# A hand-ordered attention and MLP kernel on one core: the opening and batches 1 to 4 in a new order

## The chip, the cores and the metric

The kernel runs on one core of a Trainium2 chip. The metric is device time in microseconds (us), from several executions; a profiled execution of the same program gives the trace that is read below. In a profile's lines PE is TensorE's matmul, PEld its weight load, DVE VectorE, ACT ScalarE, POOL GpSimd, and SPq the DMAs that SyncE issues.

## The reference

x is (8 batches, 8 heads, 512 tokens, 64), state (8, 8, 32, 64). Each batch and head attends both ways between tokens and state rows, and the results are joined and put through an MLP:

```
scores = scale * np.matmul(x, state.transpose(0, 1, 3, 2))
a = np.exp(scores - scores.max(-1, keepdims=True)); a /= a.sum(-1, keepdims=True) + 1e-09
xread = np.matmul(a, state)
scores2 = scale * np.matmul(state, x.transpose(0, 1, 3, 2))
a2 = ...                                  # the same softmax over the tokens
sread = np.matmul(a2, x)
y = np.concatenate([xread, sread], axis=2)   # then heads side by side: (8, 544, 512)
xn = (y - mu) / np.sqrt(var + 1e-06) * g_ln
out = y + np.maximum(xn @ w_ch1, 0.0) @ w_ch2    # 512 -> 2048 -> 512
```

## The kernel before

**Numbers.** Products run in float16 on TensorE. Each factor is split in a high and a low half (ScalarE writes the high one with an activation, VectorE the low one with one scalar_tensor_tensor), and three products of halves (TERMS) are summed. The weights come as 64-bit words, two int32 each; `words` (L653 and L697 load them, 1 MB a tile, through SyncE's queue) turns them into float32 on ScalarE and VectorE. Since xread is a product of the weights of attention with the state, the first layer is taken as state times w1 first (`state_products`, L756 for batches 0 and 1, L750 for the others; its result is the tile "matrix"), and the attention's numerators ("ea") times that.

**Batch 0** is the opening. TensorE turns x and the state (L379), scores them (L439), and ScalarE, VectorE and GpSimd take the softmax, while the weights are loaded, converted and scaled. The hidden layer is done in four units of 512 columns. `first_products` (L810) gives each unit's hidden values, `second_products_by_unit` (L824) multiplies them with that unit's w2. For units 0 to 2 the result of two of the four row blocks goes through ScalarE into a tile "part", and an accumulating DMA, issued by GpSimd, adds it to the residual xr in SBUF. There are two of these DMAs to a unit, six in all. `differences` prepares a unit's w2 for the later batches: GpSimd makes a tile d from w2h in three operations, then ScalarE and VectorE each write half of the result into w2h.

**Batches 1 to 7.** `attention(b)` loads x and state, splits x into float16 halves (tile x16, "x" in the profile) in four pieces, and turns state and x with DMA transposes that SyncE issues (sT, then xT in two halves, later ebT). `products(b)` then does the MLP with fewer, combined products (L903, L913, L961).

**Buffers.** A tag names a ring of buffers in SBUF. "quad" has two, and these serve in turn the part tiles, the tile d, and others (the state rows s_r, eB, ts, ef). "rows" and "halves" have two each. In PSUM there are four accumulators (acc), one pair of banks and two halves. A tile that takes a buffer waits until everything that used its predecessor is through, an accumulating DMA that reads it included.

**Order.** Every piece of the kernel is a generator that yields single instructions, or a group of matmuls, as closures made by `do` (L194). So nearly all instructions are recorded at L198; the matmul helpers and the loads of weights have lines of their own. The generators stand in one list of streams: 0 gain, 1 attention(0), 2 to 5 weights1 of the four units, 6 state_products(0), 7 first_products, 8 to 11 weights2, 12 to 15 sums_of_weights, 16 common_scale, 17 to 20 second_products_by_unit, 21 to 24 differences, 25 attention(1), 26 state_products(1), 27 to 30 halves_of_weights, 31 to 48 products(1), 49 attention(2), and so on to 178. PLAN (L42 to L169) is one long text of items `stream:step` or `stream:first-last`, and `issue` walks it:

```python
with tc.manual_schedule():
    for item in plan.split() or [...]:
        k, n = item.split(":")
        n = [int(v) for v in n.split("-")]
        for f in streams[int(k)][n[0]:n[-1] + 1]:
            f()
```

Each engine executes its instructions in the order in which they were issued here, and semaphore waits keep what depends on each other in order across engines. A tile gets its ring buffer where its first step stands in PLAN. So PLAN sets the order on each engine, SyncE's and GpSimd's DMAs included, and which tiles share a buffer.

Of the kernel before, what the change touches and what calls it, by code (L numbers as in the profile page):

```python
# [42 lines left out]
    "0:0 1:7 1:6 1:5 1:4 1:8 1:13 1:1 1:19 1:0 4:0 0:3 1:14 1:3 1:15 1:9 0:4 1:16 1:10 1:17 1:2 0:5 1:18 1:11 1:23 "  # L43
    "4:2 1:21-22 4:3 1:20 1:24 2:0 4:1 2:3 4:4 0:6 1:27-28 1:12 0:2 2:2 1:25 1:29 1:41 1:26 4:6 2:4 4:5 1:30 1:33 "
    "1:67 1:34 2:1 0:1 1:42 3:0 1:31 4:7 1:36 2:5 1:32 4:8 1:43-45 1:48 2:6 3:3 3:1 2:7 1:35 1:46 4:12 4:9 2:8 1:37 "
    "4:10-11 3:2 3:4 3:6 1:49 3:5 1:47 4:13 5:0 2:12 2:10 3:7 1:39 3:8 1:38 5:1 5:6 9:1 1:50 2:9 5:2 25:1 5:5 1:55 "
    "2:11 1:60 1:51 3:11 1:61 3:10 4:14 3:9 2:13 3:12 5:3 2:14 3:13 1:52 8:1 1:62 4:15 1:70 1:68 2:15 1:71-72 1:53 "
    "25:0 2:16 3:14 1:69 5:7 8:5 2:17 1:57 1:54 3:15 25:10 1:73-74 2:18 3:16 1:75 2:19 1:56 1:63-64 3:17 9:0 25:8 "
    "5:4 3:18 1:65 6:0 6:3 6:1 3:19 9:5-6 1:40 6:5 6:2 1:78 6:8 6:4 7:0 4:16 8:0 6:6 1:58 6:9 6:7 8:2 1:87 8:6 9:7 "
    "7:18 1:88 8:3 7:1 1:83 8:7 25:9 1:59 25:5 9:3 25:11 8:4 5:8 7:2 7:19 9:2 1:84 7:20 8:8 9:4 1:89 1:85 25:2 25:6 "  # L50
    "25:3 1:90 25:13 9:16 25:12 7:3 25:14 5:12 25:15 1:86 9:17 8:16 9:8 8:9 5:10 8:17-18 7:9-10 5:11 25:16 8:10-11 "
    "9:18 5:9 4:17 8:12 1:91 7:4-5 10:1 7:6 25:17 9:9 8:13 7:11 8:14 25:18 5:13 1:92 7:7 1:93 9:10 1:94 1:76 5:14 "
    "7:8 8:19 1:95 9:11 1:79 10:6 25:19 7:21 25:21 10:5 9:12 1:96 10:0 5:15 8:20 9:13 1:77 7:22 8:15 1:80-81 7:15 "
    "9:14 7:12 25:24 25:26 5:16 7:23 7:16 25:29 25:20 25:25 17:3 7:13 25:30 10:7 7:14 17:1 25:4 17:6 10:2-4 1:82 "
    "25:7 25:34 9:19 7:17 9:15 1:97 17:0 17:4 10:8 25:27 11:1 25:22 9:20 4:18 25:35 17:2 17:8 11:5 25:31 10:9 "
    "11:6-7 10:10 17:7 17:5 18:6 17:9 11:0 18:0 10:11 25:32 4:19 11:3 10:12 11:2 6:10 12:4 6:11 11:4 6:13 18:8 13:2 "
    "6:12 11:8 17:10 10:13 12:5 25:23 25:28 10:15 21:1 18:7 5:17-18 18:1 6:14 18:9 11:9-10 6:15 13:4 11:11 21:0 "
    "1:66 12:2 21:2 10:14 13:5 5:19 26:0 11:12-13 11:15 16:0-1 21:3-4 10:19 25:73 18:2 16:2 18:10 16:4 13:3 18:3 "
    "10:20 26:4 6:18 18:4 12:0 7:27 49:2 25:33 6:19 26:5 12:1 7:24 26:6 6:16 11:14 7:28-29 27:0 7:25 7:33 18:5 7:34 "
    "11:16 7:26 25:36 6:17 27:1 7:30 13:0 7:35 19:1 25:38 10:16 7:31 10:17-18 12:3 25:39 14:4 49:3 14:2 14:5 19:3 "  # L60
    "7:32 14:0 25:40 19:0 25:41-42 49:1 14:3 14:1 25:37 25:43 49:0 19:4 7:36 25:48 26:7 25:49 7:37 26:8 13:1 7:45 "
    "7:42 7:38 26:9 19:2 11:17 25:50 19:6 26:1 25:51-52 25:44 25:53 19:5 11:18 7:43 26:2 25:54 7:44 19:8 11:19-20 "
    "7:46-47 20:6 7:39 27:2 25:60-61 19:9 27:9 19:7 26:3 25:62 27:10 25:55 20:0 25:56 31:0 25:57 49:10 25:58 49:12 "
    "27:11 7:40 31:5 31:2 7:41 20:3 31:1 23:0 49:11 25:45 31:4 49:9 31:3 31:7 27:3-4 23:1 49:8 27:5 23:2 25:46 31:6 "
    "23:3-4 19:10 20:1 25:47 25:59 49:13 20:4 49:14 31:8 49:15 31:11 31:9 28:3 31:10 33:0 22:0 31:13 49:4 33:2 49:6 "
    "20:2 49:16 22:1 49:17-19 33:4 49:31 49:24 20:8 22:2 49:26 26:10 31:14 28:4 20:9 20:7 49:25 33:5 33:1 22:3 "
    "26:11 33:3 33:7 31:12 20:10 49:32 28:5 32:0 49:29-30 32:1 33:6 49:5 22:4 33:10 33:8-9 33:13 49:27 32:2 24:1 "
    "35:0 33:11 26:12 15:2 33:14 35:1 25:68 35:5 32:3 34:3 33:12 35:3 34:0 25:63 49:21 15:4 15:0 35:8 35:7 35:9 "
    "34:1 35:11 25:70 35:2 29:6 49:7 24:0 29:7 35:4 24:2 35:6 29:8 25:69 35:12 35:10 25:67 25:64 34:2 28:9-10 15:1 "
    "37:0 37:2 37:1 37:3 15:5 37:5-6 28:11 37:4 35:13 36:0 35:14 29:0 40:0 37:8 37:7 29:1 24:3 36:2-3 40:1 15:3 "  # L70
    "24:4 40:3 37:11-12 37:10 36:1 37:9 29:2 40:2 40:4 25:66 49:22 25:65 25:71 25:74 28:0 25:75 40:5 49:23 37:13-14 "
    "28:1 40:6 28:2 38:1 25:76 40:7 29:3 40:10 49:34 29:4 25:80 49:28 49:35 38:0 49:20 42:0 25:77 42:1 40:8-9 39:1 "
    "29:5 39:2 49:73 40:13-14 49:33 38:2 39:4-5 42:5 42:3 28:6 42:7 69:2 38:3 28:7 41:0 39:6 42:6 28:8 42:11 42:2 "
    "42:4 40:11-12 49:36 42:10 49:38 41:3 44:0-1 42:8-9 49:37 42:12 49:39 41:1 25:72 49:48 44:5 41:2 44:3 39:3 "
    "42:13 44:7 44:9 42:14 43:2 49:49 43:1 49:40-42 44:8 25:82-83 49:50 49:43 49:51 25:81 49:44 44:2 27:6 50:3 27:7 "
    "20:5 44:6 49:52 44:10 43:0 27:8 50:4 44:11 43:3 46:0 44:4 44:13 46:5 49:53 46:2 46:1 29:9 50:5 46:6 49:54 46:3 "
    "49:60 45:0 46:8 44:14 45:3 50:0 46:10 49:61 69:4 46:4 49:62 46:7 49:64 50:1 29:10 49:45 50:2 29:11 25:84 46:11 "
    "46:9 44:12 49:65 30:6-7 47:0 45:2 49:67 25:78 46:12-13 45:1 49:70 50:6-7 51:0-1 25:85 49:46 50:8 51:2 51:4 "
    "47:1 30:8 49:69 25:79 51:5 49:66 46:14 25:86 51:6 30:3 47:3 51:3 25:87 51:8 49:68 49:55 69:5 25:88 49:47 51:7 "
    "49:56 47:2 51:10 49:57-59 39:0 51:9 49:63 53:0 39:7 48:0 39:8 48:1 30:4 49:71 51:13 53:5 53:2 51:14 53:1 48:3 "  # L80
    "53:8 49:74 51:11 52:0 49:75 53:6 69:3 69:0 30:5 53:3 51:12 49:76 53:4 52:3 69:1 69:9 48:4 55:0 30:9 48:2 69:7 "
    "69:11 69:10 55:1 48:5 52:2 53:10 53:7 69:12 30:10 69:8 53:9 55:5 30:11 49:77 48:6 30:0 69:13-14 49:80 52:1 "
    "69:15 53:11 69:16 30:1 69:17 49:84 39:9 53:12 69:18 55:2 49:72 69:19 55:6 55:10 30:2 55:3 54:0 69:31 53:13-14 "
    "54:1 50:9 54:2 55:8 55:7 55:4 69:32 54:3 69:21 69:6 69:24 50:10 56:0 50:11 49:81 57:0 69:22 55:11 49:85 "
    "69:29-30 55:9 69:23 69:26-27 69:25 55:13 69:28 57:1-2 57:4 69:34 49:78 55:12 55:14 57:5 57:8 57:3 57:6-7 57:9 "
    "57:13 56:2 57:11 56:1 56:3 49:79 69:33 57:10 69:20 60:0 69:73 57:14 60:5 58:0 49:82 57:12 60:1 60:3 60:7 58:3 "
    "60:11-12 69:36 58:1 60:6 60:9 60:2 60:4 60:8 69:35 59:1 69:38-39 49:83 69:41 69:40 60:10 49:86-87 48:7 59:2 "
    "69:42 69:37 58:2 59:4 89:0 62:0 62:2 62:1 62:3 62:5 59:5 70:0-1 62:4 62:7 89:1 62:6 59:3 61:1 69:43 62:11 70:2 "
    "59:6 89:2 61:0 60:13-14 62:8 69:48 64:0 89:3 89:12 62:10 70:3 69:49 70:4 62:9 61:2-3 70:5 62:13 62:12 69:45 "
    "49:88 69:46 69:50-51 64:5 69:44 64:6 63:0 69:55 64:1 64:3 64:10 64:2 69:47 89:9 89:11 69:52 63:1 62:14 89:10 "  # L90
# [996 lines left out]
```

## Time and profile before

| what | value |
|---|---|
| time before, median of 3 runs | 632.94 us (632.23 to 636.33) |
| time of the profiled execution | 632.7 us |
| its span, first to last instruction | 630.9 us |
| mean granted TensorE clock | 0.99 |
| instructions | 15146 |
| DMA traffic | 60.95 MB, 97 GB/s on average |

The span is the profiled execution's own; the time has 1.8 us more. A row of a timeline has the start in us, the duration, engine and line, the operation with its output and input tiles and their shape and type, and how often it stands there back to back. In brackets is the idle time of that engine just before, and what ended it: an engine's work on a tile, or a DMA.

### The profile page before, as it was taken

Reading aid. Unit: us, or ns where it says so; the run is one execution under the profiler, and the core shown is the slowest. Engines: PE = TensorE matmul, PEld = TensorE weight load, DVE = VectorE, ACT = ScalarE, POOL = GpSimd, SP = SyncE. Lnnn points to the kernel's source line nnn. Section 1 sums busy time; section 2 is a strip of 40 time slices with the busy share of each in tenths; the row PEclk is TensorE's granted clock in tenths of the full one; section 3 lists DMA queues with packets and bytes.
Section 4 is the critical chain, followed back from the end, with each engine's and each line's share of the span. In section 5 each row is a group of like instructions: output and inputs, shape, how many; then the busy total and the mean of one; then the engine's idle time right before and its main releaser. Section 6 shows DMA issues by size and latency. Waiting matters only on the chain.

```text
span 630.9 us, 15146 instructions
## 1 busy us (share of the span) xinstructions
PE 606.1 (96%) x6232; PEld 482.7 (77%) x6232; DVE 483.0 (77%) x971; ACT 377.6 (60%) x667; POOL 231.9 (37%) x197
## 2 busy tenths in 40 slices
PE   5789979999999999999999999999999999999996
PEld 4346535568988888888888888888888888888885
DVE  2999969998898979867856797868867886665533
ACT  4999977575674946645537564655456454434332
POOL 0114133564253434344433354324442543433122
PEclk9999989999999999999999999999999999999999
DMA  8972694323524254033270433241250306201001
GB/s 297 403 251 68 213 166 110 68 43 101 85 72 104 89 99 112 18 84 63 39 208 13 89 80 84 74 91 62 59 164 14 93 14 122 72 2 35 34 34 35
DMA packets 80381, 60.95 MB, mean 97 GB/s; under 512 B 60280, under 2 KB 70776, under 8 KB 79864
## 3 DMA queue, kind: packets, MB, share of 16 engines
q1 hardware_dynamic: 77416, 56.01, 33.3%
q0 software_dynamic: 864, 3.15, 2.9%
q10 hardware_dynamic: 2032, 0.82, 0.6%
q8 instruction: 49, 0.80, 0.5%
q14 instruction: 20, 0.16, 0.1%
HBM read 28.05 MB, written 9.44 MB: 59 GB/s over the span
## 4 chain that ended last, share of the span: by engine, by line
PE 80%; DVE 2%; ACT 0%; issue 0%; DVEq 0%
PE acc L961 43%; PE half L903 23%; PE half L913 3%; PE banks L750 3%; PE acc L824 2%; PE banks L536 2%; PE banks L574 1%; PE acc L810 1%; PE banks L447 1%; PE banks L198 1%; PE banks L756 0%; DVE ts L198 0%; DVE xs L198 0%; DVE strip L198 0%; DVE mB L198 0%; DVE sums L198 0%
## 5 line engine op out<-in xcount | busy, mean ns | idle before, releaser
L961 PEld LDWEIGHTS <-xs 128*128 128x128 f16 x2520 | 243.6, 98 | 36.1 <-issue 6.4
L198 POOL TENSOR_TENSOR xs<-rs,xs 128x512 f16<-128x512 f32 x120 | 143.4, 1205 | 241.6 <-ACT xs L198 160.5
L961 PE MATMUL acc<-w2h,xs 128*128 128x256 f16 x1440 | 182.1, 273 | 0.0
L903 PE MATMUL half<-ea,matrix 128*128 128x256 f16 x1344 | 161.8, 273 | 0.1
L903 PEld LDWEIGHTS <-matrix 128*128 128x128 f16 x1344 | 129.9, 98 | 20.8 <-issue 4.1
L961 PE MATMUL acc<-sums,xs 128*128 128x256 f16 x1080 | 141.3, 273 | 0.0
L198 DVE SCALAR_TENSOR_TENSOR rs<-half,rs 128x256 f32<-128x256 f32 x224 | 89.8, 417 | 40.1 <-ACT rs L198 22.7
L198 ACT ACTIVATE xs<-rs 128x512 f16<-128x512 f32 (+1 forms) x128 | 77.6, 619 | 50.8 <-DVE rs L198 44.2
L198 ACT ACTIVATE xs<-half 128x256 f16<-128x256 f32 (+1 forms) x112 | 53.5, 485 | 54.7 <-PE half L903 20.7
L198 DVE SCALAR_TENSOR_TENSOR xs<-half,xs 128x256 f16<-128x256 f32 (+1 forms) x112 | 61.3, 549 | 23.6 <-ACT xs L198 22.1
L198 ACT ACTIVATE rs<-half 128x256 f32<-128x256 f32 x56 | 21.4, 382 | 46.4 <-PE half L903 44.2
L824 PE MATMUL acc<-w2h,hid 128*128 128x512 f16 x192 | 44.4, 388 | 0.4 <-DVE of_weights L198 0.2
L198 DVE TENSOR_TENSOR strip<-acc,strip 128x256 f32<-128x256 f32 (+1 forms) x61 | 33.3, 546 | 13.4 <-PE acc L961 8.9
L824 PEld LDWEIGHTS <-hid 128*128 128x128 f16 x192 | 19.0, 100 | 24.1 <-issue 4.3
L198 ACT ACTIVATE matrix<-banks,hs 128x1024 f16<-128x1024 f32 x24 | 26.7, 1112 | 10.0 <-PE banks L750 9.8
L198 DVE SCALAR_TENSOR_TENSOR matrix<-banks,hs,matrix 128x1024 f16<-128x1024 f32 x24 | 30.5, 1272 | 2.6 <-ACT matrix L198 2.6
L198 POOL TENSOR_TENSOR ts<-ts,mA 128x1024 f32<-128x1024 f32 (+1 forms) x8 | 15.7, 1964 | 42.4 <-DVE mA L198 30.2
L810 PE MATMUL acc<-ea,matrix 128*128 128x256 f16 x192 | 24.2, 282 | 2.6 <-DVE matrix L198 2.1
L810 PEld LDWEIGHTS <-matrix 128*128 128x128 f16 x192 | 18.6, 100 | 9.1 <-issue 3.2
L198 POOL TENSOR_TENSOR ts<-ts,dA 128x1024 f32<-128x1024 f32 (+1 forms) x8 | 15.3, 1914 | 26.7 <-DVE of_weights L198 13.4
L198 DVE SCALAR_TENSOR_TENSOR xr<-strip,of_second,xr 128x512 f32<-128x512 f32 x28 | 23.3, 840 | 0.9 <-ACT of_second L198 0.7
L198 DVE SCALAR_TENSOR_TENSOR x<-x_f,x_s,x 128x512 f16<-128x512 f32 x28 | 21.7, 791 | 2.1 <-ACT x L198 2.0
(180 smaller groups left out, 771.6 us busy)
## 6 DMA issues: line engine op xcount, KB each, us to landing
raw<-in_moe_w_ch_dram SPq DMA_DIRECT2D x10, 1024.0 KB
out_dram<-xr SPq DMA_DIRECT2D x16, 512.0 KB, 3.1
x_f<-in_x_dram SPq DMA_DIRECT2D x14, 512.0 KB
sums<-in_moe_w_ch_dram SPq DMA_DIRECT2D x6, 1024.0 KB, 9.6
ek<-ea SPq DMA_DIRECT2D x56, 64.0 KB, 2.0
ek<-ek SPq DMA_DIRECT2D x7, 512.0 KB, 4.5
xr<-part POOLq DMA_DIRECT2D x6, 512.0 KB, 4.8
s_r<-in_state_dram SPq DMA_DIRECT2D x28, 64.0 KB, 3.6
```

Source lines behind the costliest of these rows:

```text
L198: return lambda: f(*map(now, args), **{k: now(v) for k, v in kw.items()})
L447: nc.tensor.matmul(ps[32 * j:32 * j + 32, g, w * s:w * s + w], lhsT=sT[D * g:D * g + D, a, 32 * j:32 * j + 32], rhs=xT[D * g:D * g + D, k: ...
L536: nc.tensor.matmul(ps_z[:, j], lhsT=x16[:, a, i], rhs=ebT[:, k, :, c, 32 * j:32 * j + 32], start=c == 0 and n == 0, stop=c == C - 1 and n ...
L574: nc.tensor.matmul(px[:, c, D * h:D * h + D], lhsT=ek[:, h // 2, h % 2, (2 * t + c) * P:(2 * t + c + 1) * P], rhs=sk[:, h], start=True, st ...
L750: nc.tensor.matmul((ps0, ps1)[g][32 * j:32 * j + 32], lhsT=sT[D * g:D * g + D, a, 32 * j:32 * j + 32], rhs=w[D * g:D * g + D, i, j], start ...
L810: nc.tensor.matmul(o[:, 256 * f:256 * f + 256], lhsT=m[:, g, i, P * (q + f):P * (q + f) + P], rhs=ea[:, s, k, g], start=f == 0 and g == 0 ...
L824: nc.tensor.matmul(po, lhsT=hid[:, i, q, c * P:(c + 1) * P], rhs=w[:, j, q], start=first and q == 0 and n == 0, stop=last and q == 3 and n ...
L903: nc.tensor.matmul(ps[:, 256 * q:256 * q + 256], lhsT=m[:, h, i, P * (2 * k + q):P * (2 * k + q) + P], rhs=ea[:, 0, j, h, 256 * g:256 * g ...
L913: nc.tensor.matmul(ps[:, 256 * q:256 * q + 256].rearrange("p (t n) -> p t n", t=2), lhsT=w[:, i, j, fs], rhs=xsT[:, :, 4 * a + j], start=q ...
L961: nc.tensor.matmul(po[o], lhsT=y[:, n, i, o] if o < 2 else x[:, o - 2, n, i], rhs=v[j], start=u == 0 and n == 0 and k == 0 and o in (2, 1, ...
```

## The change

Only the text PLAN differs (127 lines before and after; the same 2502 steps, and the same line numbers elsewhere). The last 898 steps stand in the same order; those ahead of them are reordered: the opening, and batches 1 to 4. Of the text, two lines:

```diff
-    "0:0 1:7 1:6 1:5 1:4 1:8 1:13 1:1 1:19 1:0 4:0 0:3 1:14 1:3 1:15 1:9 0:4 1:16 1:10 1:17 1:2 0:5 1:18 1:11 1:23 "
+    "0:0 1:4-5 1:7 1:6 1:8 1:13-14 1:0 1:2 1:19 2:0 1:3 1:12 0:3 1:15 1:1 1:20 0:5 1:10 2:2-3 1:24 4:0-2 1:9 1:11 "
...
-    "6:12 11:8 17:10 10:13 12:5 25:23 25:28 10:15 21:1 18:7 5:17-18 18:1 6:14 18:9 11:9-10 6:15 13:4 11:11 21:0 "
+    "11:7 17:7 25:30 11:3 17:9 11:2 7:16 17:5 6:10 6:13 18:0 6:14 18:8 6:11 12:0 18:6 11:4 7:17 17:10 25:28 6:12 "
```

**GpSimd, from the first accumulating DMA of batch 0 on.** xr<-part are the accumulating DMAs, the first two of them unit 0's; d is the tile of differences(0). DMASW0 and DMASW1 are the semaphores of the first and the second accumulating DMA. Before:

```order
L198 DMA xr<-part 128x1024 [waits Activation_49] x2
L198 TENSOR_TENSOR d<-w2h 128x512 [waits DMASW0_49]
L198 TENSOR_TENSOR d<-w2h 128x512
L198 TENSOR_TENSOR d<-d 128x512 [waits Pool_49]
L198 DMA xr<-part 128x1024 [waits DMASW1_49,Activation_49]
L198 DMA xr<-part 128x1024 [waits Activation_49]
```

Now:

```order
L198 DMA xr<-part 128x1024 [waits Activation_49] x2
L198 TENSOR_TENSOR d<-w2h 128x512 [waits DMAHW3_49,DMAHW6_49,DMAHW1_49,DMAHW7_49,DMASW1_49,DVE_49]
L198 TENSOR_TENSOR d<-w2h 128x512
L198 TENSOR_TENSOR d<-d 128x512 [waits Pool_49]
L198 DMA xr<-part 128x1024 [waits Activation_49]
L198 DMA xr<-part 128x1024 [waits DMASW0_49,Activation_49]
```

The first operation on d waited for the first accumulating DMA and waits for the second now.

**ScalarE, unit 1's parts and what stands between them.** The first two part rows are the third pair of parts (unit 1's first), w2h<-d is the step of differences(0), and the last row is the next part. Before:

```order
L198 ACTIVATE raw,of_weights<-w_t 128x2048 [waits DVE_49]
L198 ACTIVATE part<-acc,of_unit 128x512 [waits DMASW1_49]
L198 ACTIVATE part<-acc,of_unit 128x512 [waits PE_49]
L198 ACTIVATE sums<-n_645,of_weights 128x512
L198 ACTIVATE sums<-t_618,of_weights 128x512
L198 ACTIVATE w2h<-d 128x2x256 [waits Pool_49]
L198 ACTIVATE w2h<-sums,of_weights 128x2048 [waits DVE_49]
L198 ACTIVATE part<-acc,of_unit 128x512 [waits DMASW2_49,PE_49,Activation_49]
```

Now:

```order
L198 ACTIVATE raw,of_weights<-w_t 128x2048 [waits DVE_49,Activation_49]
L198 ACTIVATE part<-acc,of_unit 128x512 [waits DMASW0_49,PE_49,Activation_49]
L198 ACTIVATE part<-acc,of_unit 128x512
L198 ACTIVATE sums<-t_490,of_weights 128x512 [waits Pool_49]
L198 ACTIVATE sums<-n_769,of_weights 128x512
L198 ACTIVATE sums<-t_598,of_weights 128x512
L198 ACTIVATE w2h<-d 128x2x256 [waits Pool_49]
L198 ACTIVATE w2h<-sums,of_weights 128x2048 [waits DVE_49]
L198 ACTIVATE part<-acc,of_unit 128x512 [waits DMASW1_49,DVE_49,PE_49]
```

The third pair of parts waited for the second accumulating DMA and waits for the first now; the next part waited for the third and waits for the second, and for VectorE.

**SyncE, batch 1's transposes of state and x.** sT and xT are the turned state and x, ebT the turned exponents. Before:

```order
L198 DMA_TRANSPOSE sT_917<-sh 128x2x128 [waits DMAHW1_49,DVE_49]
L198 DMA_TRANSPOSE xT<-x_410 128x16x128 [waits DMAHW2_49,DVE_49]
L198 DMA sread_rows<-sread 4x32x128
L198 DMA s_j<-in_state_dram 128x1x64 [waits DMAHW4_49]
L198 DMA_TRANSPOSE xT<-x_410 128x16x128 [waits DMAHW5_49]
L198 DMA s_j<-in_state_dram 128x1x64 [waits DMAHW6_49]
```

Now:

```order
L198 DMA_TRANSPOSE sT_809<-sh 128x2x128 [waits DMAHW2_49,DVE_49,Activation_49]
L198 DMA_TRANSPOSE xT<-x_351 128x16x128 [waits DMAHW3_49,DVE_49,Activation_49]
L198 DMA_TRANSPOSE xT<-x_351 128x16x128
L198 DMA s_j<-in_state_dram 128x1x64 [waits DMAHW5_49]
L198 DMA_TRANSPOSE ebT<-eb 128x16x128 [waits DMAHW6_49,DVE_49,Pool_49]
```

The store of sread and a load of state went from between the two transposes of x. In the opening, SyncE's queue also has its second half of x behind a first 1-MB tile of w1 (x_f, raw, x_f, then sums), where before both halves of x stood ahead of all weights.

250 rows, old and new, of the table PLAN are left out of this document.

## The prediction, on record before the result

> **What bounds the kernel now.** I read the page first, its busy times and the chain that ended last:
>
> ```profile
> PE 606.1 (96%) x6232; PEld 482.7 (77%) x6232; DVE 483.0 (77%) x971; ACT 377.6 (60%) x667; POOL 231.9 (37%) x197
> PE 80%; DVE 2%; ACT 0%; issue 0%; DVEq 0%
> ```
>
> TensorE is busy for 96% of the span. An order of work can therefore win only where TensorE stands still or runs slowly, so I asked next for busy times by stage. Columns: window, its length, busy us of PE, PEld, DVE, ACT and POOL, each with its count, then the granted clock, the DMA share and GB/s.
>
> ```profile
> 0.00:17.00 17.00, 9.66 (x104) 7.01 (x104) 5.43 (x13) 8.94 (x14) 0.70 (x6) 1.00 0.88 305
> 17.00:40.00 23.00, 18.64 (x148) 9.22 (x144) 21.86 (x40) 21.82 (x26) 3.12 (x2) 1.00 0.96 355
> 40.00:77.40 37.40, 34.31 (x261) 20.02 (x260) 35.51 (x78) 37.08 (x55) 9.76 (x9) 0.95 0.48 163
> 77.40:98.70 21.30, 17.91 (x104) 6.61 (x101) 14.69 (x33) 15.10 (x22) 6.95 (x6) 0.84 0.85 130
> 98.70:127.60 28.90, 28.08 (x267) 17.13 (x260) 28.29 (x33) 21.30 (x33) 14.59 (x11) 1.00 0.40 91
> 127.60:624.00 496.40, 496.20 (x5362) 421.76 (x5359) 374.11 (x771) 273.33 (x521) 196.78 (x165) 1.00 0.30 72
> 90.00:100.00 10.00, 9.52 (x58) 3.81 (x59) 7.07 (x16) 7.30 (x11) 1.65 (x3) 0.67 0.60 108
> ```
>
> From 127.6 to 624 us TensorE is idle for 0.20 us of 496.40. The reordered steps lie ahead of about 388 us, and from 127.6 us on they have nothing to give. From 98.7 to 127.6 the VectorE (28.29 of 28.90) sets the pace. From 17 to 77.4 the ScalarE or the VectorE is all but full: ScalarE has 0.32 us of idle time in 37.40. One stage is different. From 77.4 to 98.7 nothing is full: TensorE idles 3.39 us at a clock of 0.84, VectorE 6.61, ScalarE 6.20. What ends those waits is in the timelines, ScalarE, GpSimd, SyncE's queue and TensorE in turn:
>
> ```profile
> 79.19 1.25 ACT L198 ACTIVATE part<-acc,of_unit 128x512 f32<-128x512 f32 x2
> 89.49 1.27 ACT L198 ACTIVATE part<-acc,of_unit 128x512 f32<-128x512 f32 x2 [3.50 <-DMA xr<-part]
> 91.87 0.62 ACT L198 ACTIVATE w2h<-d 128x512 f16<-128x512 f32 x1
> 97.09 0.69 ACT L198 ACTIVATE part<-acc,of_unit 128x512 f32<-128x512 f32 x1 [2.70 <-DMA xr<-part]
> ```
>
> ```profile
> 77.94 1.06 POOL L198 DMA_DIRECT2D xr<-part  x1 [9.70 <-ACT part L198]
> 80.75 1.03 POOL L198 DMA_DIRECT2D xr<-part  x1 [1.76 <-ACT of_unit L198]
> 83.01 2.71 POOL L198 TENSOR_TENSOR d<-w2h 128x512 f32<-128x512 f16 x2 [1.23 <-DMA xr<-part]
> 85.80 1.27 POOL L198 TENSOR_TENSOR d<-d 128x512 f32<-128x512 f32 x1
> ```
>
> ```profile
> 80.96 2.95 SPq L198 DMA_TRANSPOSE xT<-x  x1
> ...
> 86.64 4.41 SPq L198 DMA_TRANSPOSE xT<-x  x1
> ```
>
> ```profile
> 80.66 1.09 PE L756 MATMUL acc<-w1c,sT_w 64*32 64x512 f32 x16
> ...
> 90.23 2.53 PE L756 MATMUL acc<-w1c,sT_w 64*32 64x512 f32 x16 [3.01 <-ACT part L198]
> ...
> 98.69 4.11 PE L810 MATMUL acc<-ea,matrix 128*128 128x256 f16 x36
> ```
>
> The third pair of parts on ScalarE needs a "quad" buffer that the second accumulating DMA reads. That DMA was issued at 80.75 and released ScalarE at 89.49: 8.74 us. The first, issued at 77.94, released GpSimd at 83.01: 5.07 us. The tile's own summary says the same of all six:
>
> ```profile
> DMA to landing us min/median/max: 4.5/4.8/8.7
> ```
>
> The slow one is the one whose time holds the two transposes of x. So the transposes and the accumulating DMA do slow each other here. Behind that wait, TensorE stood 3.01 us, then ran sixteen matmuls in 2.53 us that had taken 1.09, at a granted clock of 0.67.
>
> **The change part by part.** First, **the third pair of parts waits for the first accumulating DMA now**, as the rows of the change show, and the differences d on GpSimd wait for the second; the two have swapped buffers. Removed is the 3.50 us of ScalarE, with TensorE's 3.01 behind it. What is late next is d: 2.71 + 1.27 = 3.98 us on GpSimd, then w2h<-d on ScalarE (0.62), then the VectorE's half of it, behind which the whole VectorE stands in order:
>
> ```profile
> 91.40 0.75 DVE L198 SCALAR_TENSOR_TENSOR sums<-n,of_weights,sums 128x512 f16<-128x512 f32 x1 [3.79 <-ACT sums L198]
> 92.07 0.21 DVE L198 TENSOR_SCALAR of_weights<-of_weights,x_s 128x1 f32<-128x1 f32 x1
> 92.86 0.29 DVE L198 TENSOR_TENSOR sT_w<-sT 128x128 f32<-128x128 f16 x1 [0.58 <-PE acc L756]
> ...
> 94.21 0.67 DVE L198 TENSOR_TENSOR w2h<-d,w2h 128x512 f16<-128x512 f32 x1
> ...
> 99.57 2.37 DVE L198 SCALAR_TENSOR_TENSOR sums<-t,of_weights,sums 128x512 f16<-128x512 f32 x1 [0.44 <-ACT sums L198]
> ```
>
> When does the second accumulating DMA land? ScalarE has one copy less ahead of the second pair of parts (a hid<-acc, estimated from the two part copies' 1.25 us at 0.6), so the issue moves from 80.75 to about 80.1. Nothing in the new order makes SyncE wait for the accumulating DMAs: the transposes wait for x's last split on VectorE and ScalarE, which stood right ahead of 80.96 and has, by my count of the work ahead of it, hardly moved. They are now queued directly behind each other, at about 80. So I see them run with the second accumulating DMA as before, and take the row of 8.7 us. The other end is the median of 4.8.
>
> With 8.7 the landing is 88.8. d ends 3.98 later, at 92.8; with ScalarE's 0.62 and some 0.3 us of hand-overs the VectorE's w2h<-d starts at 93.7, against 94.21: 0.5 us. In front of it the VectorE has by then done the sums<-t of 2.37 us and left behind those of 0.75, 0.21 and 0.29: 1.12 us more work done. Together the VectorE, which sets the pace from 98.7 on, is **1.6 us ahead**. ScalarE's second wait, 2.70 us at 97.09, falls away too, since that part waits for the second DMA and not the third; it lies beside the VectorE's work and brings nothing of its own.
>
> With 4.8 the landing is 84.9, the VectorE's w2h<-d starts at 89.8, and the gain is 4.4 + 1.12 = 5.5 us, near the whole idle time of VectorE (6.61) and ScalarE (6.20) in this stage. I would take 4.5 of it, since the other waits of a row of dependent steps don't all vanish.
>
> Second, **the opening**. On SyncE's queue a 1-MB tile of w1 now stands between the two halves of x that SyncE loads.
>
> ```profile
> 6.99 4.87 PE L379 MATMUL acc<-idf,x_f 128*64 128x128 f32 x48 [1.00 <-DMA x_f<-in_x_dram]
> ...
> 9.02 0.60 ACT L198 ACTIVATE xT<-acc 128x512 f32<-128x512 f32 x1 [5.75 <-PE acc L379]
> 10.24 1.13 ACT L198 ACTIVATE sums<-sums 128x1024 f32<-128x1024 f32 x1 [0.63 <-DMA sums<-in_moe_w_ch_dram]
> ```
>
> At 355 GB/s, the rate from 17 to 40 us, 1.05 MB take 3.0 us. So x can be up to 3.0 us later, and the first words of w1 up to that much earlier than 10.24. ScalarE, idle until 9.02, would start with words at about 8 and turn to xT after that. It has 8.94 us of work in 17 and is full only later, so a shuffle of its first items costs little if something is there to do. Bounds: 0.8 us gained (9.02 against about 8.2), 3.0 lost. I take **0.2 lost**, nearer to the gain, because the words fill the gap.
>
> Third, **the rest of the reordered steps**, from 17 to 77 us and from 100 on, move items among engines that are already full (1.2 us of idle time on ScalarE in 17 to 40, 0.3 in 40 to 77.4). The most they can give is these 1.5 us, and a new wait could cost as much. I take 0.
>
> Sum: 1.6 gained, 0.2 lost: 1.4. The profiled execution took 632.7 us with a span of 630.9, so the time is span + 1.8. The new span is 629.5 and the time 631.3. The median of the runs shown, 632.94, is 0.2 above the profiled one, which is inside what I can tell.
>
> **The rivals.** *The transposes no longer meet the accumulating DMAs* (0.20). If x's split ends later than I count, or the second accumulating DMA starts sooner, it lands after about 4.8 us: 632.7 - 4.5 + 0.2 = 628.4. For it speaks that the two lie close, within some us; against it that no wait holds the transposes back.
>
> *The opening is late* (0.20). If the exponents' chain behind x is what ScalarE and VectorE lack between 10 and 20 us, the words of w1 don't fill the gap, and all that follows, up to 77.4 full of work, moves by the 3.0 us: 632.7 + 3.0 - 1.6 = 634.1. It decides as soon as the opening loses more than 1.6 us. Against it: the stage from 17 us on has 1.2 us of slack on either engine, and the earlier words are work that has to be done there.
>
> *The clock eats the gain* (0.15). By my estimate TensorE has finished the second products of unit 1 at about 92 and then needs sT_w, which stands behind w2h<-d on VectorE and comes at 94.7: it idles almost three us ahead of the first products of unit 2. Here is what a shorter wait did at the start of the first products, beside the clock of 0.95 in that stage:
>
> ```profile
> 45.56 2.93 PE L810 MATMUL acc<-ea,matrix 128*128 128x256 f16 x12 [2.14 <-DVE matrix L198]
> ```
>
> Twelve matmuls took 2.93 us, where 36 take 4.11 at 98.69. A stretch of 3 us at half speed costs 1.5 us if VectorE then waits for TensorE: 632.7 in all, no change. The Trainium skill's page "TensorE: Matmul & The Clock Gate", section "HAM oscillation — how this bites in real kernels", puts the abstract rule as "no PE-idle gaps >~3.4µs". By that rule a gap of almost three us would leave the clock whole, and the forecast would stand. The trace doesn't bear the rule out as a limit: its gaps of 2.14 and 3.01 us were both followed by slow matmuls.
>
> **How the numbers follow.** The forecast, that the meeting stays and only the wait is moved, has 0.45; the three rivals have 0.20, 0.20 and 0.15. The likeliest gives 631.3, by itself 630.0 to 632.6. The range reaches into the separated case to 627.0 (the 5.5 us whole would be 627.4) and over the late opening to 635.6, where the 1.5 us that the rest of the order could cost come on top. About 1% (6.3 us) is what a measurement of this kernel can tell from no change. Only the separated case with a gain in the opening comes below 626.6: 0.06. Only a late opening with a further wait comes above 639.3: 0.04. Within 1%: 0.90.
>
> **What would show it.** Right: ScalarE's third pair of parts waits for nothing or under 1 us; the second accumulating DMA is issued between 79 and 81 and takes 7 to 9 us to release GpSimd's d; both transposes start within 2 us of it; the VectorE's w2h<-d starts at 93 to 94.5, after a wait of some us for ScalarE; TensorE has its idle time ahead of batch 1's first state products (banks, L756), not ahead of unit 3's (acc, L756). The first L824 starts within 1 us of where it did. Wrong: d released 4.5 to 5.5 us after the issue (then the separation is real), or ScalarE's first work after 10 us and the first L824 over 2 us late (then the opening decides), or any wait of over 1 us behind 127.6.

## The result, and the profile after

The changed order is slower: 643.98 us median (642.43 to 644.00, 4 runs) against 633.01 (632.23 to 636.33, 4 runs), a ratio of 1.0147 (95% interval 1.0115 to 1.0179). By the medians that is 11.0 us; by the ratio it is 9.3 (7.3 to 11.3). The profiled execution took 642.43 us, 9.7 us more than the one before, with a span of 640.4. The busy times by stage, in the same windows and columns as before:

```profile
0.00:17.00 17.00, 8.20 (x71) 6.52 (x71) 2.28 (x6) 5.68 (x8) 0.70 (x6) 1.00 0.87 310
17.00:40.00 23.00, 16.87 (x88) 7.40 (x90) 18.45 (x34) 19.70 (x25) 2.10 (x2) 0.85 0.80 299
40.00:77.40 37.40, 31.32 (x309) 19.32 (x308) 36.05 (x83) 37.20 (x55) 9.00 (x8) 0.91 0.54 175
77.40:98.70 21.30, 20.90 (x127) 9.22 (x126) 18.74 (x38) 20.34 (x29) 6.59 (x6) 1.00 0.76 160
98.70:127.60 28.90, 26.64 (x212) 14.61 (x210) 27.40 (x31) 19.09 (x29) 12.85 (x9) 0.94 0.42 95
127.60:624.00 496.40, 492.39 (x5338) 416.41 (x5337) 377.28 (x770) 272.61 (x520) 196.93 (x163) 1.00 0.29 72
```

Read down the columns against those of before. By 40 us VectorE has done 20.73 us of work and not 27.29, ScalarE 25.38 and not 30.76: the opening is some 6 us behind. From 40 to 77.4 both are full, as before, and catch nothing up. In the stage of the stall VectorE does 18.74 us and not 14.69, TensorE 20.90 at a full clock and not 17.91 at 0.84: 3 to 4 us come back. Then TensorE loses again: 26.64 and not 28.08 up to 127.6, and 4.01 us of idle time behind it where there were 0.20.

**The opening.** ScalarE with its queue, VectorE and TensorE:

```profile
12.41 0.28 ACT L198 ACTIVATE sT_w<-banks 128x128 f32<-128x128 f32 x1 [8.17 <-PE banks L198]
12.66 0.38 ACTq L198 DMA_DIRECT2D gx<-in_moe_g_ln_dram  x1
```

```profile
22.25 0.17 DVE L198 TENSOR_SCALAR gm<-gx 128x4 f32<-128x4 f32 x1 [3.24 <-DMA gx<-in_moe_g_ln_dram]
```

```profile
9.90 1.97 PE L379 MATMUL acc<-idf,x_f 128*64 128x128 f32 x14 [3.45 <-DMA x_f<-in_x_dram]
...
23.25 1.11 PE L439 MATMUL banks<-xT,sT_w 64*32 64x256 f32 x16 [4.30 <-DVE ts L198]
```

Two things stand late. ScalarE's first copy, sT_w, waits 8.17 us for a small matmul that stands behind a turn of x on TensorE, and that turn waits for x. And the load of the gain gx, 2 KB, is now issued at 12.66 us and not at 2.77, and gm, which needs it, comes at 22.25 and not at 13.84, with VectorE and then TensorE behind it. On the chain that ended last the load stands with its whole time:

```profile
12.66 9.57 DMA gx<-in_moe_g_ln_dram
```

**The stall.** GpSimd, SyncE's queue and ScalarE:

```profile
85.83 0.87 POOL L198 DMA_DIRECT2D xr<-part  x1 [3.20 <-ACT part L198]
91.08 2.58 POOL L198 TENSOR_TENSOR d<-w2h 128x512 f32<-128x512 f16 x2 [4.39 <-DMA xr<-part]
```

```profile
86.78 7.07 SPq L198 DMA_TRANSPOSE xT<-x  x2
```

```profile
91.67 1.26 ACT L198 ACTIVATE part<-acc,of_unit 128x512 f32<-128x512 f32 x2
```

The second accumulating DMA releases d 5.25 us after its issue. SyncE issued the first transpose 0.95 us after that DMA, but the two did not move data together. All that the core's DMA engines carried from 86 to 90 us are the accumulating DMA's 128 packets of 4 KB (a packet is one of the pieces in which the profile counts a transfer); the transposes' packets, of 256 bytes, come from 90.14 us on. From 86 to 90 us (queue, packets, MB, share of the 16 engines):

```profile
q0 software_dynamic: 128, 0.52, 78.6%
```

The slowest of the six accumulating DMAs takes 5.1 us (8.7 before). The third pair of parts waits for nothing.

**Behind 127 us.** GpSimd, VectorE, ScalarE and TensorE:

```profile
141.01 0.89 POOL L198 DMA_DIRECT2D xr<-part  x1
```

```profile
145.65 0.75 DVE L198 SCALAR_TENSOR_TENSOR xr<-acc,of_unit,xr 128x512 f32<-128x512 f32 x1 [3.62 <-DMA xr<-part]
```

```profile
146.91 0.72 ACT L198 ACTIVATE x<-x_f,x_s 128x512 f16<-128x512 f32 x1 [4.38 <-DVE x_s L198]
```

```profile
150.34 0.39 PE L961 MATMUL acc<-w2h,xs 128*128 128x256 f16 x2 [1.00 <-ACT xs L198]
```

The sixth accumulating DMA is issued at 141.01, behind a difference of the next unit on GpSimd. VectorE adds unit 3's products to the same xr and waits for it; ScalarE, GpSimd and TensorE wait behind VectorE.

### The profile page after: what moved, and what is told of

Same layout as the page of the kernel before. It is cut to its first block, busy times and chain, and to the rows that moved or that the text cites. A ratio compares the mean times of both kernels' runs of the same rounds, so it can differ in the third digit from the quotient of the medians.

```text
span 640.4 us, 15133 instructions
## 1 busy us (share of the span) xinstructions
PE 607.1 (95%) x6229; PEld 482.9 (75%) x6232; DVE 486.3 (76%) x971; ACT 378.6 (59%) x667; POOL 232.2 (36%) x197
## 4 chain that ended last, share of the span: by engine, by line
PE 77%; DVE 8%; ACT 7%; DMA 3%; issue 3%; POOL 2%; ACTq 0%; POOLq 0%; DVEq 0%
PE acc L961 41%; PE half L903 22%; PE half L913 3%; PE banks L750 3%; PE acc L824 2%; ACT raw L198 2%; DMA gx<-in_moe_g_ln_dram 1%; PE banks L536 1%; DMA x_f<-in_x_dram 1%; DVE w1c L198 1%; POOL d L198 1%; PE banks L447 1%; ACT sums L198 1%; PE banks L574 1%; DVE sums L198 1%
## 5 line engine op out<-in xcount | busy, mean ns | idle before, releaser
L961 PEld LDWEIGHTS <-xs 128*128 128x128 f16 x2520 | 243.6, 98 | 38.3 <-issue 6.8
L198 POOL TENSOR_TENSOR xs<-rs,xs 128x512 f16<-128x512 f32 x120 | 144.2, 1210 | 258.3 <-ACT xs L198 177.2
L961 PE MATMUL acc<-w2h,xs 128*128 128x256 f16 x1440 | 182.5, 273 | 2.3 <-POOL xs L198 1.3
L961 PE MATMUL acc<-sums,xs 128*128 128x256 f16 x1080 | 141.7, 273 | 0.0
L198 DVE SCALAR_TENSOR_TENSOR rs<-half,rs 128x256 f32<-128x256 f32 x224 | 90.1, 417 | 39.7 <-ACT rs L198 17.2
L198 ACT ACTIVATE xs<-rs 128x512 f16<-128x512 f32 (+1 forms) x128 | 77.8, 618 | 54.8 <-DVE rs L198 45.4
L198 ACT ACTIVATE xs<-half 128x256 f16<-128x256 f32 (+1 forms) x112 | 53.1, 485 | 61.8 <-DVE rs L198 20.7
L198 DVE SCALAR_TENSOR_TENSOR xs<-half,xs 128x256 f16<-128x256 f32 (+1 forms) x112 | 61.3, 549 | 21.4 <-ACT xs L198 18.9
L824 PE MATMUL acc<-w2h,hid 128*128 128x512 f16 x192 | 43.3, 379 | 1.1 <-DVE w2h L198 1.1
L198 DVE TENSOR_TENSOR strip<-acc,strip 128x256 f32<-128x256 f32 (+1 forms) x61 | 33.3, 547 | 12.1 <-PE acc L961 8.9
L198 ACT ACTIVATE rs<-half 128x256 f32<-128x256 f32 x56 | 21.3, 380 | 34.7 <-PE half L903 32.5
L824 PEld LDWEIGHTS <-hid 128*128 128x128 f16 x192 | 18.4, 98 | 24.2 <-issue 3.9
L198 POOL TENSOR_TENSOR ts<-ts,mA 128x1024 f32<-128x1024 f32 (+1 forms) x8 | 16.8, 2103 | 51.4 <-DVE mA L198 51.4
L198 ACT ACTIVATE matrix<-banks,hs 128x1024 f16<-128x1024 f32 x24 | 26.6, 1110 | 13.2 <-PE banks L750 13.0
L198 DVE SCALAR_TENSOR_TENSOR matrix<-banks,hs,matrix 128x1024 f16<-128x1024 f32 x24 | 30.4, 1267 | 3.8 <-ACT matrix L198 3.8
L198 DVE SCALAR_TENSOR_TENSOR xr<-strip,of_second,xr 128x512 f32<-128x512 f32 x28 | 24.1, 865 | 1.0 <-ACT of_second L198 0.7
L198 ACT ACTIVATE x<-x_f,x_s 128x512 f16<-128x512 f32 x28 | 18.8, 712 | 9.8 <-DVE x_s L198 9.8
L198 DVE SCALAR_TENSOR_TENSOR x<-x_f,x_s,x 128x512 f16<-128x512 f32 x28 | 22.0, 805 | 2.3 <-ACT x L198 1.9
```

What stands on the lines that cost most here:

```text
L198: return lambda: f(*map(now, args), **{k: now(v) for k, v in kw.items()})
L824: nc.tensor.matmul(po, lhsT=hid[:, i, q, c * P:(c + 1) * P], rhs=w[:, j, q], start=first and q == 0 and n == 0, stop=last and q == 3 and n ...
L961: nc.tensor.matmul(po[o], lhsT=y[:, n, i, o] if o < 2 else x[:, o - 2, n, i], rhs=v[j], start=u == 0 and n == 0 and k == 0 and o in (2, 1, ...
```

## The experiments

All kernels compute the reference's whole result; they differ in PLAN alone. Their text has one or two lines less, so L197 there (L196 in e4) is L198 here. Times are medians, ratios are to the kernel before on the same chip; the runs were spread over several chips.

| run | time, us | ratio (95% interval) |
|---|---|---|
| e1, gain loaded early | 638.32 | 1.0080 (1.0057 to 1.0103) |
| e2, turn of x later | 637.77 | 1.0074 (1.0049 to 1.0099) |
| e3, old opening, new rest | 645.37 | 1.0184 (1.0160 to 1.0209) |
| e4, new opening, old rest | 644.83 | 1.0180 (1.0158 to 1.0202) |
| e5, before, split of x later | 629.84 | 0.9948 (0.9924 to 0.9971) |
| e6, e2 with the split earlier | 642.90 | 1.0152 (1.0124 to 1.0181) |
| e7, e2 with the sixth DMA earlier | 634.76 | 1.0020 (1.0001 to 1.0040) |
| e8, e7 with the matrix earlier | 632.01 | 0.9979 (0.9964 to 0.9995) |
| e9, halves of x together | 642.62 | 1.0130 (1.0086 to 1.0175) |
| e10, before, gain loaded late | 638.74 | 1.0076 (1.0053 to 1.0099) |
| e11, before, split one step later | 630.48 | 0.9939 (0.9916 to 0.9962) |
| e12, all of it | 631.77 | 0.9959 (0.9935 to 0.9984) |

**The load of the gain (e1).** Step 0:5 is the load of gx.

```diff
-1:3 1:12 0:3 1:15 1:1 1:20 0:5 1:10
+1:3 0:5 1:12 0:3 1:15 1:1 1:20 1:10
```

> The changed order, with one step moved: the load of the gain gx stands on ScalarE's queue right behind its two loads of x, as it did before the change, and no longer behind the copy sT_w. Theory A (the opening loses the time: ScalarE's first copy, sT_w, stands behind a turn of x on TensorE that waits for x until 9.9 us, and all else stands behind that copy, the load of gx included): gm no longer holds VectorE until 22.25 us, the waits of 3.24 us on VectorE, 4.30 on TensorE and 3.30 on ScalarE there go, about 3 us are gained, time near 641. Rival B (the opening's delay would be taken up in the idle stage around 80 to 98 us, and the time is lost by the new order behind 98 us): no change, 644.

638.32: 5.7 us less than the changed kernel, and more than theory A gave it. ScalarE's queue, ScalarE and VectorE:

```profile
2.78 0.52 ACTq L197 DMA_DIRECT2D gx<-in_moe_g_ln_dram  x1
12.69 0.28 ACT L197 ACTIVATE sT_w<-banks 128x128 f32<-128x128 f32 x1 [7.87 <-PE banks L197]
```

```profile
18.73 0.15 DVE L197 TENSOR_SCALAR gm<-gx 128x4 f32<-128x4 f32 x1
```

gm waits for nothing now. But sT_w is as late as in the changed kernel, and still 5.7 us came back. So that copy, which theory A put first, is not what costs the time.

**The turn of x (e2).** Step 1:12 is the turn, 1:20 the copy sT_w.

```diff
-1:3 1:12 0:3 1:15 1:1 1:20 0:5 1:10
+1:3 0:3 1:15 1:1 1:20 1:12 0:5 1:10
```

> The changed order, with one step moved: the first turn of x on TensorE stands behind the copy sT_w in the order, so that the small matmul on which sT_w waits stands ahead of it on TensorE. Theory A: sT_w goes from 12.4 us to about 6, the words of w1 start at about 8 and not at 13.1, gx is loaded six us earlier; 4 to 6 us are gained, time 638 to 640. Rival B: the opening is earlier, the time stays within 1 us of 644.

637.77. It looks like theory A, but gx stands behind sT_w here and goes earlier with it:

```profile
6.03 0.28 ACT L197 ACTIVATE sT_w<-banks 128x128 f32<-128x128 f32 x1 [1.76 <-PE banks L197]
6.03 0.42 ACTq L197 DMA_DIRECT2D gx<-in_moe_g_ln_dram  x1
8.91 2.13 ACT L197 ACTIVATE raw<-raw 128x1024 f32<-128x1024 f32 x2 [2.60 <-DMA raw<-in_moe_w_ch_dram]
```

The copy comes 6.4 us earlier than in the changed kernel, yet the gain over e1 is 0.6 us, well inside both intervals. Both runs have in common that gx is early.

**The load of the gain, late in the kernel before (e10).**

```diff
-1:2 0:5 1:18 1:11 1:23 4:2 1:21-22 4:3 1:20 1:24
+1:2 1:18 1:11 1:23 4:2 1:21-22 4:3 1:20 0:5 1:24
```

> The order of before, with one step moved: the load of the gain gx stands behind the copy sT_w on ScalarE, as in the changed order. Theory A: issued at about 12.8 us beside the loads of the weights, its 512 packets of 4 bytes take some 9 us, VectorE stands at gm until about 22 and not 13.8, the first means of w1 on TensorE (17.0 us) wait for it: 5 to 7 us lost, 638 to 640. Rival D: what waits for gm has other work beside it: 633 to 635.

638.74, as theory A had it. ScalarE's queue, VectorE and TensorE:

```profile
10.57 0.37 ACTq L197 DMA_DIRECT2D gx<-in_moe_g_ln_dram  x1
```

```profile
20.04 0.17 DVE L197 TENSOR_SCALAR gm<-gx 128x4 f32<-128x4 f32 x1 [6.00 <-DMA gx<-in_moe_g_ln_dram]
```

```profile
21.16 1.11 PE L438 MATMUL banks<-xT,sT_w 64*32 64x256 f32 x16 [6.03 <-DVE ts L197]
```

One load of 2 KB, put some 8 us later, costs 5.5 us (638.74 against 633.22 on that chip) in a kernel in which nothing else is moved. From issue to use it takes 9.5 us here and 9.6 in the changed kernel. It is no quicker when it is issued early: in the kernel before, a load of SyncE's queue that waits for it goes out at 13.40, 10.6 us after the issue at 2.77. So a later issue is a later landing.

**The halves of x (e9).** Step 1:1 is SyncE's second half of x, 2:0 the 1-MB tile.

```diff
-2:0 1:3 1:12 0:3 1:15 1:1 1:20 0:5
+1:1 2:0 1:3 1:12 0:3 1:15 1:20 0:5
```

> The changed order, with one step moved: SyncE's second half of x stands ahead of the first 1-MB tile of w1, as before the change; the turn of x and the load of gx stay where the change has them. Theory A (the rings of SyncE and ScalarE take turns packet by packet, and the tile's 4-KB packets hold up ScalarE's 512-byte packets of x): TensorE's wait of 3.45 us for x shrinks to under 1, sT_w goes from 12.4 us to about 9.5, and the whole opening comes 2.5 to 3 us earlier: 640 to 641.5. Rival D (only the order on TensorE and ScalarE matters, x would be late anyway): within 1 us of 644.

642.62, 1.4 us less, between the two. The intervals of this ratio and of the changed kernel's overlap widely, so it can't be told from no change. TensorE and ScalarE:

```profile
7.65 1.97 PE L378 MATMUL acc<-idf,x_f 128*64 128x128 f32 x14 [1.07 <-DMA x_f<-in_x_dram]
```

```profile
10.17 0.28 ACT L197 ACTIVATE sT_w<-banks 128x128 f32<-128x128 f32 x1 [5.91 <-PE banks L197]
12.75 0.38 ACTq L197 DMA_DIRECT2D gx<-in_moe_g_ln_dram  x1
```

x comes 2.25 us earlier, about as theory A said, and ScalarE's copy too. But gx is issued at 12.75 all the same: it also waits for the semaphore of another load, which it takes over. The chain that ended last has that load of sums right ahead of it:

```profile
3.23 9.50 DMA sums<-in_moe_w_ch_dram
12.75 9.47 DMA gx<-in_moe_g_ln_dram
```

gm stands at 22.24, and with that the earlier x can bring little.

**Old opening with the new rest, and the other way (e3, e4).**

```diff
-PLAN of the changed kernel
+first 270 steps of before, then the changed order's remaining steps (e3); and the reverse (e4)
```

> The first 270 steps (to about 67 us) in the order of before, all others in the changed order. Theory A: the 7 us that TensorE had lost more at 68 us are not lost; the later new waits (about 3 us at 104 to 110, about 3 at 144 to 152) remain, the stall at 85 to 98 is shorter; time 631 to 635. Rival B: the loss is behind 98 us: 640 to 644.

> The first 270 steps in the changed order, all others in the order of before. Theory A: the opening's 7 us come on top, less what the idle stage around 80 to 98 us takes up (up to 3): 636 to 640. Rival B: that stage takes up all: 633 to 634.

645.37 and 644.83: e3 speaks for neither theory as it was put, and e4 is slower than both gave it. GpSimd and SyncE's queue in e3, then its slowest accumulating DMA:

```profile
85.32 0.87 POOL L197 DMA_DIRECT2D xr<-part  x1 [4.03 <-ACT part L197]
```

```profile
85.41 9.95 SPq L197 DMA_TRANSPOSE xT<-x  x2
```

```profile
DMA to landing us min/median/max: 4.5/4.9/9.1
```

The same in e4:

```profile
87.06 1.08 POOL L196 DMA_DIRECT2D xr<-part  x1 [0.85 <-ACT of_unit L196]
```

```profile
87.35 3.79 SPq L196 DMA_TRANSPOSE xT<-x  x1
```

```profile
DMA to landing us min/median/max: 4.5/4.6/14.2
```

The cut moves the later meeting. In e3, with the very order in which the two kept apart, the transposes come 0.09 us after the second accumulating DMA and not 0.95, and it takes 9.1 us; e4 has 0.29, where the kernel before has 0.21, and 14.2 us, and TensorE waits 6.6 us for the parts. e3 has a wait of its own besides, 4.1 us of TensorE for VectorE's hid soon behind the place where the two orders join. So these two can't weigh the opening against the rest. What they show is that no wait keeps the transposes and the DMA apart in the changed kernel: it is a matter of when x's split ends.

**The meeting itself (e5, e11, e6).** Step 25:32 is the last split of x in the order of before; 11:3 and 11:4 are a conversion.

```diff
-25:32 4:19 11:3 10:12 11:2 6:10 12:4 6:11 11:4
+4:19 11:3 10:12 11:2 6:10 12:4 6:11 11:4 25:32
```

> The order of before, with one step moved: VectorE's last split of x for batch 1 stands two splits later, behind w_t<-raw of unit 3, so that the first transpose of x is issued some 3 us after batch 0's second accumulating DMA and not 0.2 us after it. Theory A (what decides is which starts first: an accumulating DMA that has begun about a microsecond ahead runs undisturbed, and one that begins with the transposes takes 8 to 14 us): the second accumulating DMA takes about 5 us and not 8.7, ScalarE's wait of 3.5 us and TensorE's of 3.0 shrink to under 1, time 629 to 631. Rival C (they share the DMA engines whenever they overlap, so that the later start only shifts it): it takes 7 us or more, time 632 to 633.

629.84, the lowest median of all. GpSimd, SyncE's queue and TensorE:

```profile
80.99 0.86 POOL L197 DMA_DIRECT2D xr<-part  x1 [1.75 <-ACT of_unit L197]
```

```profile
84.82 1.82 SPq L197 DMA_TRANSPOSE xT<-x  x1
```

```profile
88.26 1.09 PE L755 MATMUL acc<-w1c,sT_w 64*32 64x512 f32 x16
```

The second accumulating DMA takes 4.7 us. The matmuls that had waited 3.01 us and taken 2.53 at 90.23 now wait for nothing, take 1.09, and stand 2 us earlier. One step moved in VectorE's order gives 3.2 us (interval 1.8 to 4.8, by the ratio).

```diff
-25:32 4:19 11:3 10:12
+4:19 11:3 25:32 10:12
```

> The order of before, with VectorE's last split of x one step later and not two, so that the first transpose is issued about 1 us behind the second accumulating DMA. Theory A (a microsecond is enough): the second accumulating DMA takes 5.0 to 5.5 us, the time is within 1 us of the run with the split two steps later, 629 to 631. Rival C: 6.5 us or more, 631.5 to 633.

630.48: one step is enough. The first transpose comes 0.93 us after the DMA (84.31 and 85.24), and the DMA takes 5.3 us.

Then the other way, in e2 (25:30 is the last split in its order, 11:7 the conversion):

```diff
-11:7 17:7 25:30 11:3
+25:30 11:7 17:7 11:3
```

> The kernel of the run with the turn of x later, with one more step moved: VectorE's last split of x stands ahead of a conversion of 1.2 us, so that the transposes are issued at or just before the second accumulating DMA and not 0.95 us after it. Theory A: the second accumulating DMA takes 8 to 14 us and not 5.1, d and all of VectorE behind it come 3 to 9 us late, time 641 to 646. Rival C: about the same as without the move, 637 to 639.

642.90, 5.1 us more than e2. GpSimd and SyncE's queue:

```profile
81.94 0.86 POOL L197 DMA_DIRECT2D xr<-part  x1 [3.20 <-ACT part L197]
89.70 2.71 POOL L197 TENSOR_TENSOR d<-w2h 128x512 f32<-128x512 f16 x2 [6.90 <-DMA xr<-part]
```

```profile
81.72 8.30 SPq L197 DMA_TRANSPOSE xT<-x  x2
```

Issued 0.22 us behind the transposes, the DMA releases d after 7.76 us and not 5.24 as in e2. The size is below the 8 to 14 that theory A gave, the time is as it said. Rival C's time, 637 to 639, is missed, and its picture of two transfers that share the engines does not fit e2: there, as in the changed kernel, the DMA's 128 packets run alone (82.4 to 85.5 us). In e6 the transposes' packets run alone from 82.9 to 85.2 us, and the DMA's first comes at 85.28.

**The sixth accumulating DMA (e7).** Step 19:10 is that DMA, 23:0 the first operation of differences(2); everything between them stays.

```diff
-25:47 23:0
...
-20:8 19:10 31:8
+25:47 19:10 23:0
...
+20:8 31:8
```

> The kernel of the run with the turn of x later, with one more step moved: GpSimd issues the sixth accumulating DMA ahead of the differences of unit 2 and not behind them and one more. Theory A (behind 140 us VectorE's first addition to xr waits 3.6 us for this DMA, and ScalarE, GpSimd and TensorE behind it): that wait goes, TensorE's waits of 1.3 and 1.0 us in L961 go, time 634.5 to 636. Rival B' (those waits have other causes and only change their name): 637 to 638.5.

634.76, 3.0 us less than e2, as theory A had it. The DMA is issued at 125.95, and VectorE's wait for it and TensorE's two in L961 are gone:

```profile
125.95 0.89 POOL L197 DMA_DIRECT2D xr<-part  x1 [2.58 <-ACT z L197]
```

**Batch 1's first matrix (e8).** 26:5 and 26:6 are its two halves, 13:1 and 12:3 the splits of sums.

```diff
-13:1 12:3 49:2 6:17 26:5 7:27-28 7:30 26:6
+26:5 13:1 26:6 12:3 49:2 6:17 7:27-28 7:30
```

> The run before with two more steps moved: batch 1's first matrix goes ahead of a split of sums of 2.4 us on VectorE, and ahead of it on ScalarE. Theory A (TensorE's wait for the scores of batch 1, 2.3 us with a half clock behind it, is the place of that step in VectorE's order): the wait goes, 2 to 3 us gained, time 631.5 to 633.5. Rival: VectorE is full there, and the wait moves to the products that need the split: within 1 us of the run before.

632.01, 2.75 us less than e7. TensorE's scores of batch 1 in e7, then in e8:

```profile
101.56 0.84 PE L446 MATMUL banks<-xT,sT 64*32 64x512 f16 x24 [2.26 <-DVE ux L197]
```

```profile
99.72 0.84 PE L446 MATMUL banks<-xT,sT 64*32 64x512 f16 x24
```

The 5.8 us from e2 to e8 are surer than their parts. e7's ten executions spread from 632.64 to 636.28, and the two profiled ones, 632.84 and 632.19, are only 0.65 us apart. One reason shows in the traces of e2 and e7: both have the wait for the scores, 2.27 and 2.26 us, and the 36 matmuls behind it take 5.30 us in e2 and 4.10 in e7, at a mean granted clock of 0.94 and 1.00 from 98.7 to 127.6 us:

```profile
103.30 5.30 PE L809 MATMUL acc<-ea,matrix 128*128 128x256 f16 x36
```

```profile
102.33 4.10 PE L809 MATMUL acc<-ea,matrix 128*128 128x256 f16 x36
```

So the same wait drew a slow clock behind it in one execution and not in the other.

**All of it (e12).** e8 with e1's and e9's moves.

```diff
-1:19 2:0 1:3 0:3 1:15 1:1 1:20 1:12 0:5
+1:19 1:1 2:0 1:3 0:5 0:3 1:15 1:20 1:12
```

> The changed order with all that was found put right: the turn of x behind sT_w, the load of gx behind the loads of x, both halves of x ahead of the weights, the sixth accumulating DMA ahead of the differences, batch 1's first matrix earlier. Theory A (these are the places of the loss, and each was paid by itself): the opening is as early as before's, the collision stays away, 628.5 to 631. Rival: what is gained in the opening is waited for later: 631.5 to 632.5, as without the two loads moved.

631.77: the rival's number. With the turn later, gx was early enough; the two loads add nothing that can be told from 632.01. It beats the kernel before by 0.4%. e5, one step moved, is 1.9 us faster by the medians, which come from two chips; by the ratios it is 0.7 us, and their intervals overlap. Whether the changed order loses anything else is open.

## Why the prediction was wrong

The sign was wrong, and 643.98 lies outside the range. All of the prediction's own signs of being wrong came: d released 5.25 us after the issue; ScalarE's first copy at 12.41 us and the first L824 at 72.18 and not 66.87; and a wait of 3.62 us behind 127.6.

**What failed first is the opening's term, "0.2 lost".** It was made from x and the tile of w1 alone. The change also moved a load of 2 KB on ScalarE's queue from 2.77 us to behind the copy sT_w, and the prediction didn't cost it, although a moved step's DMAs count. By itself it costs 5.5 us (e10 against before) or 5.7 (the changed kernel against e1). Moving the halves of x together again gave 1.4 us while gx stayed late, which is not clear of noise (e9), and 0.2, with a still earlier gx, once gx was early (e12 against e8). "The words fill the gap" failed as well: ScalarE takes its instructions in order, and the copy ahead of the words held them until 12.41. That hold was real but nearly free (e1). The rival of the late opening had the place and the sign right. Its mechanism, x, was wrong, and so was its price of 3.0 us.

**"I see them run with the second accumulating DMA as before, and take the row of 8.7 us"** failed. The first transpose was issued 0.95 us behind the DMA and not 0.21 as before, the DMA's packets were through before the transposes' first, and it took 5.1 us. The first rival, the separated case, was right in the DMA's time and in the separation: x's split ended later beside the DMA than I counted. That no wait holds the transposes back, which stood against it, is right too: a microsecond's difference brings the collision (e3, e6). Keeping the two apart is worth 3.2 us (e5), and bringing them together in e2 costs 5.1 (e6). The forecast had 8.7 and 4.8 as bounds and took the wrong one.

**"The rest of the reordered steps: I take 0"**, with 1.5 us at most, failed twice: 3.0 us for the sixth accumulating DMA's place on GpSimd's queue (e7) and 2.75 for batch 1's first matrix on VectorE (e8), by the medians; 5.8 together. "From 127.6 us on they have nothing to give" was right, and hid that they had something to take: a stage that is full before can still get a new wait.

**What held:** the third pair of parts waits for nothing, and d is next on the path; VectorE and ScalarE pass a delay in the opening on nearly whole (in e10 a wait of 6.0 us for gx, 5.5 us of time). The third rival, the clock, did not come where it was put: from 77.4 to 98.7 us the granted clock was 1.00, and 0.84 before.

**The account.** Put right one after the other, the three places give back 6.2 (e2), 3.0 (e7) and 2.75 us (e8): 12.0, which is all of the 11.0 that were lost and 1.0 more. If the transfers kept apart are worth the 3.2 us of e5 in the new order too, 2.2 us are still lost somewhere. The intervals of e5 and e8 overlap, so these 2.2 may be noise; no run settles it.

## What to carry to other kernels

Cost every DMA that a reordering moves by when it is issued and what else the queues carry then, the small ones first: 2 KB beside a stream of weights took 9.5 us. If an order keeps two transfers apart by timing alone, ask what holds it: here another order ahead of about 67 us cut a lead of 0.95 us to 0.09 and brought the collision back (e3). Moving one step at a time out of a large reordering showed a version (e5) that beats both.

## What the runs showed of the hardware

**An accumulating DMA and DMA transposes: whose packets start first.** Delay of the first transpose behind the DMA's issue, and the time to landing of the slowest accumulating DMA: -0.22 us, 7.6 (e6); 0.09, 9.1 (e3); 0.21, 8.7 (before) and 8.6 (e10); 0.29, 14.2 (e4); 0.95, 5.1 (changed kernel). In e11 and e5, at 0.93 and 3.83 us, the second DMA takes 5.3 and 4.7, and the slowest is the third. It is issued while the first transpose's packets still run, and 0.40 and 0.67 us ahead of the second transpose: 7.3 and 6.5. GpSimd and SyncE's queue in e11:

```profile
91.18 0.88 POOL L197 DMA_DIRECT2D xr<-part  x1 [0.74 <-ACT part L197]
```

```profile
91.58 6.57 SPq L197 DMA_TRANSPOSE xT<-x  x1
```

Undisturbed ones take 4.5 to 5.1 us. The packets divide the runs. In e6, e3, e4, e10 and the kernel before, the first transpose's packets start ahead of the second DMA's. In the kernel before, the transposes' packets are all that moves from 82.6 to 83.7 us, and the DMA's, issued at 80.75, come from 83.75 to 88.8 with transposes' packets between them:

```profile
q1 hardware_dynamic: 802, 0.21, 108.3%
```

In the changed kernel, e2, e11 and e5 the DMA's packets are all through before the transposes' first. That one comes 3.4 us after its issue in the changed kernel (86.78 and 90.14), and 1.2 us after it in e5, where the DMA is through by then, and in e6, where the DMA's first packet comes late instead: 3.3 us after its issue, and 1.4 in the changed kernel. So there the later of the two waits; what holds it back, and why the two mix in the kernel before, no run shows.

**A small load beside large ones.** gx, 2.0 KB, took 9.5 us (e10) and 9.6 (changed kernel) from issue to use, beside 1-MB loads of weights, and 10.6 us in the kernel before. The Trainium skill's page "DMA: Bandwidth & Descriptors", section "Queues, rings and completion order", says that an engine takes turns between its rings a whole packet at a time. That fits: from gx's first packet to its last in the changed kernel, 16.27 to 21.68 us, ScalarE's queue (q10) moved 527 packets of 4 bytes and SyncE's (q1) 544 packets, 512 of them of 4 KB, about one for one. (The page's packet may hold several of the pieces that the profile counts, so the fit is a loose one.)

```profile
q1 hardware_dynamic: 544, 2.10, 99.2%
q10 hardware_dynamic: 527, 0.00, 6.0%
```

The packets' size was not varied, so that the size makes the load slow is argued and not shown. The 3.6 us from the issue to the first packet are not explained.
